# Which groups take the second level of a fast matrix scheme, and where their chains begin: a change to a pooled-attention and snake-MLP kernel

## The chip, the cores and the metric

The kernel runs on one core of a Trainium2 chip. The metric is the device time of one execution in microseconds (us), the median of several runs. The kernel before takes 938.45 us (three runs, 937.84 to 940.55).

The engines named in this document are TensorE (PE in the profile, its weight loads PEld), VectorE (DVE), ScalarE (ACT), GpSimd (POOL) and SyncE (SP, which issues nearly all transfers). [...]

## The reference

Attention with keys and values that are pooled by eight, and behind it two matrix products with a "snake" activation between them. All tensors are float32.

```python
# q, k, v: (8, 8, 576, 64)
k_p = k.reshape(B, H, Sp, 8, D).mean(axis=3)          # 72 pooled keys
v_p = v.reshape(B, H, Sp, 8, D).mean(axis=3)
attn = softmax(q @ k_p.T / sqrt(D))
x = (attn @ v_p)                                       # as 4608 tokens of 512
h = x @ w_in                                           # w_in: 512 x 2048
s = sin(alpha * h)
g = h + s * s / (alpha + 1e-9)
out = g @ w_out                                        # w_out: 2048 x 512
```

## The kernel before

The tokens are handled in nine **units** of 512 (u = 0 to 8). In each unit the product `x @ w_in` is taken as a 2 x 2 block product by a scheme that needs seven products instead of eight. The 2048 columns are taken in four **groups** (J = 0 to 3), and a group goes through seven **slots** (k = 0 to 6) with the products 1, 5, 6, 2, 7, 3, 4. One product is four matmuls of 128 x 128 by 256 columns. TensorE accumulates the scheme's sums in four PSUM banks of the group, b1, b6, b5, b7; copies on ScalarE carry a partial sum from one bank to the next (b1 to b6, b6 to b7), and additions on VectorE close the four results.

Beside this the attention of the next batch is spread over the slots as "extras": scores, shifts (maximum and subtraction, VectorE), exponentials (ScalarE), normalisation (VectorE sums, GpSimd multiplies), turning of blocks by 32 x 32 transposes (VectorE) and moves by SyncE.

In units 1 to 6 (`two`) some products go through **the scheme a second time**: product 5 in groups 1, 2 and 3, and product 1 in group 3. Such a product is seven matmuls of 128 columns where the plain form has four of 256, and needs three copies on ScalarE and one addition on VectorE of its own:

```python
def a():
    products((1, 5), (y[:, 0], y[:, 1]), True)                    # TensorE, into bank y
    nc.scalar.copy(out=f[:, 0], in_=y[:, 0:1].to_broadcast([P, 2, P]))
    m5[p] = self.sm.tile([P, 1, P], F32, name=f"m{p}", bufs=1)
    nc.scalar.copy(out=m5[p][:], in_=y[:, 1:2])
def b():
    products((6, 2), (c[1], c[0]))
    nc.scalar.copy(out=c[2], in_=c[1])
def d():
    products((7,), (c[2],))
    nc.vector.tensor_tensor(out=f[:, :, 1], in0=x, in1=m5[p][:].to_broadcast([P, 2, P]), op=OP.add)
def e():
    products((3, 4), (c[1], c[2]))
```

The parts of a group that the steps below follow, in the order of the program (G is this group, Q the one in front of it, N the next one when it is begun early, which is so for group 3; cuts are marked):

```python
if k == 0:
    ...
        self.last_sines(Q, 2 if not inner else 0)
    extras()
    ...
    if G.i5: G.i5.a()
    if G.i1: self.last_sines(Q, 0)
    else:
        product(G, 1, G.b1, True)
        if G.i5: product(Q, 4, Q.b7, part=(2, 3))
elif k == 1:
    if not G.i1: copy(G.b6[:], G.b1[:])
    if G.i5 and not G.i1:
        self.last_sines(Q, 1); G.i5.b()
    ...
    extras()
    if not G.i5: product(G, 5, G.b5, True)
...
elif k == 3:
    copy(G.b7[:], G.b6[:])
    G.p5 = self.tp.tile([P, JW, TH], F32, name="p5")
    if not G.i5: copy(G.p5[:], G.b5[:])
    else:
        if G.i1: squares(Q, 0)
        squares(Q, 1)
        G.i5.d()
        self.finish(Q); self.store_g(Q)
    extras()
    product(G, 2, G.b1)
    if G.i1: G.i5.e(); copy(G.p5[:], G.b5[:])
elif k == 4:
    sin(G, 0, 0, G.b1)
    ...
    extras()
    product(G, 7, G.b7, part=(0, 1))
    if G.i5:
        if not G.i1: G.i5.e(); copy(G.p5[:], G.b5[:])
        square(G, 0, 0)
    product(G, 7, G.b7, part=(2, 3))
elif k == 5:
    add(G.g[:, 1, :, 1], G.b7[:], G.p5[:])       # VectorE: reads b7 and p5
    extras()
    ...
    product(G, 3, G.b6)
else:
    add(G.g[:, 0, :, 1], G.b6[:], G.p5[:])
    sin(G, 1, 1, G.g[:, 1, :, 1])
    last()                                       # VectorE: b1 + s
    extras()
    product(G, 4, G.b7, part=(0, 1))             # writes b7 again
    ...
```

In units 1 to 6 the extras of group 1 hold the exponentials (slots 8, 9, 10, 10), the normalisations (10, 10, 11, 12) and the turns (12, 12, 13, 13). The extras of group 3 hold the turning of a later batch's q (`turn_q`: parts 0 and 1 on VectorE in slots 22 and 23, parts 2 and 3 as transfers in 24 and 25) and the attention's product with the values (`all_values`, slot 25).

Of the kernel before, what the change touches and what calls it, by code (L numbers as in the profile page):

```python
# [40 lines left out]
class Kernel:  # L41
# [704 lines left out]
    def inner_w_in(self):  # L746

        w = self.q_tile(0)[:]
        at = 0
        for p, J0 in ((5, 1), (1, 3)):  # L750
            n = self.NJ - J0
            A = self.A[p][:].rearrange("p k (J j m) -> p k J j m", j=2, m=P)[:, :, J0:]
            L = lambda i, j: A[:, j, :, i]
            s1, s2, s3, s4 = (w[:, at + i * n * P:at + (i + 1) * n * P].rearrange("p (J m) -> p J m", m=P) for i in range(4))
            at += 4 * n * P
            self.sums(((s1, L(1, 0), L(1, 1), OP.add), (s2, s1, L(0, 0), OP.subtract), (s3, L(0, 0), L(1, 0), OP.subtract), (s4, L(0, 1), s2, OP.subtract)))
            self.W2[p] = J0, {1: L(0, 0), 2: L(0, 1), 3: s4, 4: L(1, 1), 5: s1, 6: s2, 7: s3}
# [25 lines left out]
    def hidden(self, u, extra):  # L783

        nc = self.nc
        add = lambda o, x, y: nc.vector.tensor_tensor(out=o, in0=x, in1=y, op=OP.add)  # L786
        copy = lambda o, x: nc.scalar.copy(out=o, in_=x)  # L787
        sin, square, early = self.sin, self.square, lambda G: G.J == (0 if G.u else 1)
        two = 0 < u < self.B - 1

        def begin(J):

            b1, b6, b5, b7 = (self.bank([P, JW, TH]) for _ in range(4))
            new = lambda n, **kw: self.hp.tile([P, 2, JW, 2, TH], F32, name=n, **kw)
            G = SimpleNamespace(u=u, J=J, b1=b1, b5=b5, b6=b6, b7=b7, g=new("h"), s=self.s,
                                p5=None, i1=None, i5=None, early=J == (0 if u else 1))
            if two and J > 0:
                G.i5 = self.inner_product(G, 5, b5, 7)
            if two and J == 3:
                G.i1 = self.inner_product(G, 1, b1, 6)  # L800
            return G

        def product(G, p, ps, start=False, part=range(4)):

            xT, bt = self.xT[G.u], self.bt[G.u]
            B = lambda i, j: xT[:, 2 * i:2 * i + 2, j * TH:(j + 1) * TH]
            x = {1: B(0, 0), 2: B(1, 0), 3: B(1, 1), 4: bt[:, 3], 5: bt[:, 0], 6: bt[:, 1], 7: bt[:, 2]}[p]
            for n in part:
                jj, kk = divmod(n, 2)
                f = G.J * JW + jj  # L810
                nc.tensor.matmul(ps[:, jj, :], self.A[p][:, kk, f * P:(f + 1) * P], x[:, kk, :],  # L811
                                 start=(start and n == 0), stop=(kk == 1), skip_group_check=True)

        def squares(Q, i):

            if i == 0 and not Q.early:
                square(Q, 0, 1)
            if i == 1:
                square(Q, 1, slice(0, 2))

        self.squares = squares
        for slot in range(7 * self.NJ):
            J, k = divmod(slot, 7)
            Q, G = self.before, self.group

            def extras():
                for f in extra[slot]:
                    f()

            if k == 0:  # L830
                Q = self.before = G
                N = self.next
                inner = N or (two and J > 0)
                if Q and not N:
                    self.last_sines(Q, 2 if not inner else 0)
                extras()
                G = self.group = N or begin(J)
                self.next = None
                if G.i5:
                    G.i5.a()  # L840
                if G.i1:
                    self.last_sines(Q, 0)
                else:
                    product(G, 1, G.b1, True)
                    if G.i5:
                        product(Q, 4, Q.b7, part=(2, 3))
            elif k == 1:
                if not G.i1:
                    copy(G.b6[:], G.b1[:])
                if G.i5 and not G.i1:  # L850
                    self.last_sines(Q, 1)
                    G.i5.b()
                if Q and not G.i1:
                    squares(Q, 0)
                    if not G.i5:
                        squares(Q, 1)
                extras()
                if not G.i5:
                    product(G, 5, G.b5, True)
            elif k == 2:  # L860
                if Q and not G.i5:
                    self.finish(Q)
                extras()
                if G.i1:
                    product(G, 6, G.b6, part=(0, 1))
                    G.i5.b()
                    self.last_sines(Q, 1)
                    product(G, 6, G.b6, part=(2, 3))
                else:
                    product(G, 6, G.b6)  # L870
            elif k == 3:
                late = J == 0 and two
                if Q and not late and not G.i5:
                    self.store_g(Q)
                copy(G.b7[:], G.b6[:])
                G.p5 = self.tp.tile([P, JW, TH], F32, name="p5")
                if not G.i5:
                    copy(G.p5[:], G.b5[:])
                else:
                    if G.i1:  # L880
                        squares(Q, 0)
                    squares(Q, 1)
                    G.i5.d()
                    self.finish(Q)
                    self.store_g(Q)
                extras()
                product(G, 2, G.b1)
                if G.i1:
                    G.i5.e()
                    copy(G.p5[:], G.b5[:])  # L890
            elif k == 4:
                sin(G, 0, 0, G.b1)
                if not G.i5:
# [4 lines that stand above are left out]
                    if not G.i1:  # L898
                        G.i5.e()
                        copy(G.p5[:], G.b5[:])  # L900
# [3 lines that stand above are left out]
                add(G.g[:, 1, :, 1], G.b7[:], G.p5[:])  # L904
                extras()
                N = None
                if two and J + 1 == 3:
                    N = self.next = begin(J + 1)
                    N.i1.a()
                product(G, 3, G.b6, part=(0, 1))  # L910
                if N:
                    N.i1.b()
                product(G, 3, G.b6, part=(2, 3))
            else:
                if J == 0 and two and Q:
                    self.store_g(Q)
                add(G.g[:, 0, :, 1], G.b6[:], G.p5[:])
                sin(G, 1, 1, G.g[:, 1, :, 1])
                N = self.next
                last = lambda: add(G.g[:, 0, :, 0], G.b1[:], G.s[:, 0, :, 0])  # L920
                if not N:
                    last()
                    extras()
                    product(G, 4, G.b7, part=(0, 1))
                    if not (two and J < 3):
                        product(G, 4, G.b7, part=(2, 3))
                else:
                    product(G, 4, G.b7, part=(0,))
                    N.i1.d()
                    last()  # L930
                    product(G, 4, G.b7, part=(1, 2))
                    N.i1.e()
                    copy(N.b6[:], N.b1[:])
                    extras()
                    product(G, 4, G.b7, part=(3,))
# [165 lines left out]
    def carry(self, u):  # L1101
# [3 lines left out]
        at = lambda slot, f, *a: x[slot].append(lambda: f(*a))  # L1105
        last = self.B - 1
        b = u + 1
        if u == 0:
            A0, A = self.att[:2]
# [43 lines left out]
            turn = 23  # L1153
# [3 lines left out]
        if 0 < u < last:  # L1157
            A = self.att[b]
# [2 lines left out]
            at(6, A.two_shifts)  # L1161
            for i in range(4):
                at((8, 9, 10, 10)[i], A.exp, i)
                at((10, 10, 11, 12)[i], A.norm, i)
                at((12, 12, 13, 13)[i], A.turn, i)
            at(14, A.move, range(4))
            at(6, self.load_v, b)
# [11 lines left out]
            turn = 22  # L1179
        elif u:  # L1180
            turn = None
        if turn and u + 2 <= last:
            for part in range(4):
                at(turn + part, self.turn_q, u + 2, part)
        if u + 1 < self.NU:
            at(27, self.sums_of_x, u + 1, 0)
            at(27, self.sums_of_x, u + 1, 1)
# [325 lines left out]
```

## Time and profile before

| | |
|---|---|
| time | 938.45 us (937.84 to 940.55) |
| span of the profiled execution | 938.6 us |
| TensorE matmuls busy | 910.1 us, 97% |
| VectorE busy | 678.7 us, 72% |
| ScalarE busy | 452.0 us, 48% |
| GpSimd busy | 205.7 us, 22% |
| mean TensorE clock granted | 0.991 of full speed |

In the trace a matmul of 128 x 128 by 256 float32 columns leaves two matmul records, so a product of four matmuls appears as "x8". A record's own duration is longer than its share of a stream[...]; the pace is read from the start of one group of records to the start of the next. In a timeline line the first number is the start in us from the span's start, the second is how long the merged group took, and the bracket says how long the engine sat idle in front of it and what released it.

The units with the second level lie between about 91 us and 452 us of the span; one of them takes some 60 us (product with the next scores begins at 94.54, 154.82, 215.43 and 276.27 us).

### The profile page before, as it was taken

How to read it: one execution, taken by the hardware profiler on the slowest of the kernel's cores; microseconds unless marked ns; L12 is line 12 of the kernel's file. 1: busy time of each engine (PE TensorE's matmuls, PEld its weight loads, DVE VectorE, ACT ScalarE, POOL GpSimd, SP SyncE). 2: the span in 40 equal slices, each digit the busy share in tenths (PEclk: the TensorE clock that was granted, in tenths of full speed). 3: DMA queues.
4: the chain of work that ended last, by engine and by line, in shares of the span. 5: the costliest groups of instructions: out<-in, count | busy, mean ns of one | idle time of the engine just before them, and what ended most of it. 6: DMA issues, size and time to landing. Idle time of an engine off the chain costs nothing.

```text
span 938.6 us, 18229 instructions
## 1 busy us (share of the span) xinstructions
PE 910.1 (97%) x7146; PEld 821.0 (87%) x7146; DVE 678.7 (72%) x1030; ACT 452.0 (48%) x1070; POOL 205.7 (22%) x215
## 2 busy tenths in 40 slices
PE   8999999999998999999999999999999999999997
PEld 5787778788777787778888899999999999999997
DVE  6685666656767467564446889988889798989795
ACT  5686665866667767666796641212111111211111
POOL 4788352624624346231000000000000000000000
PEclk9999999999999999999999999999999999999999
DMA  9965766757647575444725445353435444352501
GB/s 247 241 192 154 194 167 182 179 167 173 198 148 200 166 184 159 148 147 120 258 90 168 163 141 162 92 164 90 157 97 136 118 127 128 112 142 90 163 15 38
DMA packets 134796, 141.15 MB, mean 150 GB/s; under 512 B 49896, under 2 KB 103288, under 8 KB 134712
## 3 DMA queue, kind: packets, MB, share of 16 engines
q1 hardware_dynamic: 132536, 138.03, 51.9%
q10 hardware_dynamic: 2176, 1.97, 0.8%
q8 instruction: 57, 0.93, 0.4%
q14 instruction: 27, 0.22, 0.1%
HBM read 75.37 MB, written 47.19 MB: 131 GB/s over the span
## 4 chain that ended last, share of the span: by engine, by line
PE 79%; ACT 7%; DVE 4%; DMA 3%; SPq 3%; issue 2%; POOL 1%; ACTq 0%; DVEq 0%; POOLq 0%
PE PS L1258 40%; PE PS L811 31%; PE PS L971 2%; PE PS L291 2%; SPq L492 2%; PE PS L579 2%; ACT s L948 1%; ACT s L941 1%; ACT ex L340 1%; DMA a<-in_moe_w_in_dram 1%; DMA h<-in_v_dram 1%; DVE h L993 1%; PE PS L592 1%; ACT L340 1%; DVE h L786 1%
## 5 line engine op out<-in xcount | busy, mean ns | idle before, releaser
L811 PE MATMUL PS<-home,a 128*128 128x256 f32 x1104 | 267.3, 388 | 14.9 <-DVE h L786 13.8
L811 PEld LDWEIGHTS PS<-home,a 128*128 128x128 f32 x1104 | 206.6, 194 | 51.7 <-DVE h L786 16.6
L811 PE MATMUL PS<-home,as 128*128 128x256 f32 x720 | 171.4, 382 | 0.4 <-ACT PS L787 0.4
L811 PEld LDWEIGHTS PS<-home,as 128*128 128x128 f32 x720 | 132.5, 190 | 18.2 <-issue 1.3
L1258 PE MATMUL PS<-s,wb 128*128 128x144 f32 x896 | 119.3, 286 | 0.4 <-ACT PS L1378 0.4
L1258 PEld LDWEIGHTS PS<-s,wb 128*128 128x128 f32 x896 | 113.7, 190 | 0.7 <-ACT PS L1378 0.6
L948 ACT ACTIVATE s<-s,c 128x256 f32<-128x256 f32 (+1 forms) x216 | 111.2, 579 | 0.0
L786 DVE TENSOR_TENSOR h<-PS,p 128x512 f32<-128x512 f32 x72 | 49.1, 683 | 73.1 <-PE PS L811 44.1
L941 ACT ACTIVATE s<-h,al 128x256 f32<-128x256 f32 x144 | 65.6, 510 | 58.5 <-DVE h L786 55.0
L122 POOL TENSOR_TENSOR kvin<-kvin 96x768 f32<-96x768 f32 (+3 forms) x42 | 72.4, 1724 | 70.6 <-DMA kvin<-in_v_dram 68.9
L1378 ACT COPY PS<-PS 128x144 f32<-128x144 f32 x56 | 14.7, 263 | 145.7 <-PE PS L1258 144.3
L1258 PE MATMUL PS<-r,wb 128*128 128x144 f32 x512 | 73.2, 286 | 0.0
L1258 PE MATMUL PS<-s,a 128*128 128x144 f32 x512 | 73.2, 286 | 0.0
L993 DVE TENSOR_TENSOR h<-PS,s 128x512 f32<-128x512 f32 x36 | 24.8, 688 | 64.2 <-ACT s L948 64.2
L941 ACT ACTIVATE s<-PS,al 128x256 f32<-128x256 f32 x144 | 60.3, 471 | 21.9 <-PE PS L811 20.4
L1258 PEld LDWEIGHTS PS<-r,wb 128*128 128x128 f32 x512 | 67.1, 190 | 0.1
L1258 PEld LDWEIGHTS PS<-s,a 128*128 128x128 f32 x512 | 67.0, 190 | 0.0
L787 ACT COPY PS<-PS 128x512 f32<-128x512 f32 x72 | 41.4, 575 | 39.1 <-PE PS L811 28.2
L1397 ACT COPY PS<-PS 128x144 f32<-128x144 f32 x56 | 14.7, 263 | 88.4 <-PE PS L1258 88.4
L1258 PE MATMUL PS<-s,we 128*128 128x144 f32 x384 | 54.9, 286 | 0.0
L1258 PE MATMUL PS<-x,wb 128*128 128x144 f32 x384 | 54.9, 286 | 0.0
L993 DVE TENSOR_TENSOR h<-h,s 128x1024 f32<-128x1024 f32 x36 | 51.0, 1417 | 0.0
(214 smaller groups left out, 1397.8 us busy)
## 6 DMA issues: line engine op xcount, KB each, us to landing
g_bridge<-h SPq DMA_DIRECT2D x72, 512.0 KB
r<-g_bridge SPq DMA_DIRECT2D x31, 1152.0 KB
out_dram<-o SPq DMA_DIRECT2D x124, 72.0 KB
kvin<-in_k_dram SPq DMA_DIRECT2D x14, 576.0 KB
q<-in_q_dram SPq DMA_DIRECT2D x7, 1024.0 KB
kvin<-in_v_dram SPq DMA_DIRECT2D x14, 512.0 KB
aM<-tr SPq DMA_DIRECT2D x54, 92.0 KB
aM<-tr SPq DMA_DIRECT2D x54, 88.0 KB
```

The source lines that it names most:

```text
L122: self.nc.gpsimd.tensor_tensor(out=t[..., 0:w] if w > D else out, in0=t[..., 0:w], in1=t[..., w:2 * w], op=OP.add)
L291: nc.tensor.matmul(ps[e][r0 + r:r0 + r + q.shape[-1], h, :], q[s], kb[s, hp, :], start=True, stop=True)
L340: nc.scalar.activation(out=E(i), in_=E(i), func=AF.Exp, scale=scale)
L492: queue.dma_start(out=self.aM[r:r + 32, a, 0:w], in_=tr[32 * a:32 * a + 32, c, s, 0:w])
L579: nc.tensor.matmul(o[r:r + 64], w, x, start=start and i < 2, stop=False, skip_group_check=True)
L786: add = lambda o, x, y: nc.vector.tensor_tensor(out=o, in0=x, in1=y, op=OP.add)
L787: copy = lambda o, x: nc.scalar.copy(out=o, in_=x)
L811: nc.tensor.matmul(ps[:, jj, :], self.A[p][:, kk, f * P:(f + 1) * P], x[:, kk, :], start=(start and n == 0), stop=(kk == 1), skip_group_ch ...
L941: self.nc.scalar.activation(out=G.s[:, i, jj, j, :], in_=src[:, jj], func=AF.Sin, scale=self.al[:, f:f + 1])
L948: self.nc.scalar.activation(out=x, in_=x, func=AF.Square, scale=self.c[:, f:f + 1])
L993: add = lambda o, x, y: self.nc.vector.tensor_tensor(out=o, in0=x, in1=y, op=OP.add)
L1258: nc.tensor.matmul(out, W[:, J // 2, J % 2, :], A[:, J, :], start=(start and J == 0), stop=(J == self.NJ - 1), skip_group_check=True)
```

## The change

The change has five parts.

1. **Group 1 of units 1 to 6 goes back to the plain form of product 5.** Only groups 2 and 3 keep the second level. The sums of the weights for it are made for two groups instead of three.
2. **What hangs on it in group 0 and group 1:** the second half of product 4 of group 0 stays in its own slot 6 and is no longer put behind product 1 of group 1; the last sines of group 0 all come in slot 7; product 5's copy into `p5` comes in slot 10, ahead of that slot's extras.
3. **One normalisation is begun a slot earlier** (the first in slot 9 instead of 10).
4. **Product 5's chain of group 3 begins in group 2:** step a in slot 20, between parts of product 4 of group 2; b in slot 21, d in slot 23 between the halves of product 6, and e where it was, behind product 2.
5. **The turning of q stands behind the addition of step d:** both VectorE parts in slot 23, and that slot's extras behind d.

Parts 1 to 3 take the second level's copies and late closing out of the group that also carries the exponentials; parts 4 and 5 are to keep the closing of product 5 in group 3 from standing behind the transposes of q.

```diff
@@ inner_w_in
-        for p, J0 in ((5, 1), (1, 3)):
+        for p, J0 in ((5, 2), (1, 3)):
@@ begin(J)
-            if two and J > 0:
+            if two and J > 1:
                 G.i5 = self.inner_product(G, 5, b5, 7)
@@ k == 0
-                inner = N or (two and J > 0)
                 if Q and not N:
-                    self.last_sines(Q, 2 if not inner else 0)
+                    self.last_sines(Q, 0 if two and J == 2 else 2)
                 extras()
                 G = self.group = N or begin(J)
                 self.next = None
-                if G.i5:
-                    G.i5.a()
                 if G.i1:
+                    G.i5.b()
                     self.last_sines(Q, 0)
                 else:
+                    if G.i5:
+                        G.i5.a()
                     product(G, 1, G.b1, True)
@@ k == 2
-                extras()
+                if not G.i1:
+                    extras()
                 if G.i1:
                     product(G, 6, G.b6, part=(0, 1))
-                    G.i5.b()
+                    G.i5.d()
+                    extras()
                     self.last_sines(Q, 1)
                     product(G, 6, G.b6, part=(2, 3))
@@ k == 3
                     squares(Q, 1)
-                    G.i5.d()
+                    if not G.i1:
+                        G.i5.d()
                     self.finish(Q)
@@ k == 6
                     product(G, 4, G.b7, part=(0, 1))
-                    if not (two and J < 3):
+                    if not (two and J == 1):
                         product(G, 4, G.b7, part=(2, 3))
                 else:
                     product(G, 4, G.b7, part=(0,))
                     N.i1.d()
                     last()
+                    N.i5.a()
                     product(G, 4, G.b7, part=(1, 2))
@@ carry: the extras of units 1 to 6
-                at((10, 10, 11, 12)[i], A.norm, i)
+                at((9, 10, 11, 12)[i], A.norm, i)
@@ carry: turning of q
-                at(turn + part, self.turn_q, u + 2, part)
+                at(((turn, turn + 1) if u == 0 else (23, 23))[part] if part < 2 else turn + part, self.turn_q, u + 2, part)
```

## The prediction

> **What bounds the kernel now.** I read the page first. TensorE's matmuls are busy for 910.1 us of 938.6, so about 28 us are open gaps. A second loss hides inside the busy time: the mean granted clock is 0.991. Then I asked who ends TensorE's waits. One line carries half of the gaps.
>
> ```profile
> L811 PE MATMUL PS<-home,a 128*128 128x256 f32 x1104 | 267.3, 388 | 14.9 <-DVE h L786 13.8
> ```
> ```profile
> PE PS L811 <- DVE h L786: 13.8, 7, 2.3
> PE PS L971 <- DVE PS L986: 2.4, 2, 1.4
> ```
>
> The second fence is the list of TensorE's waits: us in total, times, longest. The reader is to see that 13.8 us come in seven waits, the longest 2.3. In the timeline of TensorE alone, six of them are exactly 2.25 us, at 117.51, 177.79, 238.40, 299.25, 359.22 and 419.78 us: one in each of units 1 to 6, always ahead of the first half of product 4 in group 1. The seventh is 0.26 us in unit 0. So this is one place in the program, not jitter. The timeline of all engines in unit 2 shows the chain:
>
> ```profile
> 170.74 0.58 ACT L787 COPY PS<-PS 128x512 f32<-128x512 f32 x1
> 171.25 1.33 ACT L948 ACTIVATE s<-s,c 128x512 f32<-128x512 f32 x2
> 172.49 1.48 ACT L340 ACTIVATE ex<-ex 128x576 f32<-128x576 f32 x2
> ...
> 173.99 1.28 ACT L941 ACT_TABLE_LOAD   x1
> ...
> 175.28 0.84 ACT L941 ACTIVATE s<-PS,al 128x256 f32<-128x256 f32 x2
> ...
> 176.01 0.58 ACT L787 COPY p<-PS 128x512 f32<-128x512 f32 x1
> ...
> 177.04 0.69 DVE L786 TENSOR_TENSOR h<-PS,p 128x512 f32<-128x512 f32 x1
> ```
>
> Read it backwards. Product 4 writes b7, so it waits for the addition b7 + p5 (177.04). That waits for the copy into p5 (176.01). The copy stands in ScalarE's order behind two exponentials, a table load and two sines, because step e of the second level ends only in slot 11. ScalarE is 48% busy over the span, but in this stretch it is full: 12.85 us busy of 15.80 (162.00 to 177.80). The bound here is ScalarE's order, although the page calls the kernel TensorE bound.
>
> The wait has a tail. Two stretches right behind it, in units 1 and 2, from one table by stretches (columns: length, busy time of PE, PEld, DVE, ACT, POOL, then the clock):
>
> ```profile
> 117.50:122.00 4.50, 4.17 (x20) 3.40 (x20) 4.47 (x10) 2.06 (x6) 2.67 (x3) 1.00 1.03 275
> 177.80:183.50 5.70, 5.70 (x21) 4.91 (x22) 5.67 (x14) 2.82 (x7) 3.79 (x4) 0.70 0.88 230
> ```
>
> In unit 2 the clock behind the wait is 0.70 in the mean, which is 0.30 x 5.70 / 0.5 = 3.4 us at half speed. From the start of that product 4 to step b of group 2 it takes 183.47 - 177.79 = 5.68 us; in unit 1 it takes 122.06 - 117.51 = 4.55, of which 0.39 is a further wait. The slow clock costs 5.68 - 4.16 = 1.52 us. Units 3, 5 and 6 look like unit 2 (5.69, 5.62, 5.67), unit 4 like unit 1.
>
> In group 3 step e waits for the addition of step d, which stands behind the transposes of q, and these wait for a move to free their buffer (unit 1):
>
> ```profile
> 136.48 3.02 DVE L214 STREAM_TRANSPOSE tr<-q 128x1024 f32<-128x1024 f32 x4 [3.28 <-DMA aM<-tr]
> ...
> 139.88 0.49 PE L971 MATMUL PS<-home,q 128*128 128x128 f32 x2 [1.38 <-DVE PS L986]
> ```
>
> [...] Here the load takes 1.28 us and the sines start right behind it (173.99 to 175.28)[...]. [...]
>
> **The change part by part.** Paces first: 16 records of 128x256 take 3.45 us from start to start (87.46 to 90.94, less a few ns), so 0.216 us a record; a pair of 128-column records takes 0.222 us.
>
> *Product 5 of group 1.* Plain: 8 x 0.216 = 1.73 us. Second level: 7 x 0.222 = 1.55. All of it lies on TensorE's path: +0.18 us a unit, +1.1 us in six.
>
> *Removed from ScalarE in group 1:* copies of 0.36, 0.26 and 0.28 us, on the chain; from VectorE, one addition of 0.43.
>
> *The chain of group 1 anew, on unit 2's clock,* from the start of product 4 of group 0 at 163.16. TensorE without waits: product 4 to 164.89, product 1 to 166.62, 5 to 168.35, 6 to 170.08, 2 to 171.81, 7 to 173.54, 3 to 175.28. ScalarE, by the steps between starts in the trace: sines at 164.08 (they wait for the addition at 163.36, which does not move), square 164.90, sines of b7 165.70, copy to b6 when product 1 has landed, 166.85, squares 167.33, table load 168.57, first two exponentials 169.85, copy to b7 171.01 to 171.59, p5 to 172.0, the third exponential to 172.7, the fourth to 173.5. So b7 is ready for product 7 (171.81). VectorE: the third normalisation's sum waits for 172.7 and ends at 173.6; the addition b7 + p5 waits for product 7 (about 173.74) and ends at 174.43. TensorE wants b7 at 175.28: **the wait is gone with 0.85 us to spare**.
>
> *Into group 2.* In unit 1 step b waits for a copy that comes 5.26 us after that addition began (116.80 to 122.06). Now 173.74 + 5.26 = 179.00, and TensorE arrives at 175.28 + 3.89 = 179.17: the 0.39 wait goes too. The copy to b6 ends about 0.1 us late for product 6, at 179.7.
>
> *Sum of the stretch* from product 4 of group 0 to product 6 of group 2. Before: 19.87 us (unit 1), 20.75, 20.76, 19.88, 20.71, 20.75. After: 72 records x 0.216 + 4 pairs x 0.222 + 0.1 = 16.5. Saved 3.3 us twice and 4.2 four times: 23.5 us, the 1.1 already paid. Four slow-clock stretches of 1.52 are 6.1 of it; six waits of 2.25 are 13.5; the rest is small stalls.
>
> *Group 3.* From product 4 of group 2 to product 7 of group 3 the units take 12.61, 12.17, 12.20, 12.30, 12.17 and 12.17 us before. The step-e wait (1.38 in unit 1, 1.07 in unit 4, 0.44 on the weight loads in unit 5) disappears: step d's addition now ends at about 5.0 us after that product 4 begins, and step e arrives at 7.0. But the next limit is close. The product with the values needs the bank that VectorE's `finish` reads, and in unit 2 its weight load waits 1.02 us for it:
>
> ```profile
> 201.15 0.20 PEld L579 LDWEIGHTS PS<-aM,vm 64*64 64x64 f32 x4 [1.02 <-DVE h L993]
> ```
>
> `finish` waits for the squares. I put these at 8.2 us after product 4 begins, since the copy to b7 comes 0.1 later than before; the transposes of q, now behind the addition, end at 5.0 + 3.02 = 8.0. So group 3 takes about 12.3 us everywhere: -0.3 in unit 1, +0.1 in four. **I count zero.** GpSimd's weight sums for group 1 are hidden.
>
> **The rivals.** *The exponentials become the limit of b7's addition through VectorE.* The normalisations stand ahead of the addition. If the third exponential ends a microsecond later than I chain it, product 4 waits 0.2 us or more a unit; an ideal 23.5 becomes 19 only if that is 0.75 us in every unit. For: ScalarE stays full in group 1. Against: the move of one normalisation to slot 9 and three copies fewer. *The slow clock stays.* If it belonged to phases of the run and not to the wait, 6 us stay lost and the result is 921. Against: it appears only behind the wait. *Group 3 pays it back.* If the move of the blocks lands 1 us later against TensorE, `finish` and the values slip in five units: 5 us, 921. Against: the turns on VectorE begin 0.7 us earlier against TensorE than before. *Only the matmuls count:* +1.1 us, 939.5; the six waits speak against it.
>
> **Range and chances.** The ideal is 938.45 - 23.5 = 915. I allow 0.25 us a unit for stalls that the chain does not show: 1.5 us, so **916.5 us**. One rival coming true gives about 921, two give 925; the best case with group 3 also shorter is 913. I take 913 to 922 as the range of 8 in 10. Faster by over 2% means below 919.7: 0.8; within 2%: 0.19; slower: 0.01.
>
> **What would show it.** In the changed profile the wait of product 4 on the addition should have left the list of TensorE's waits; the granted clock of units 1 to 6 should be 1.00 in every stretch, the mean near 0.998 (0.991 plus 4 x 3.4 x 0.5 / 938.6); one unit should take 57 us instead of 60.5; the p5 copy of group 1 should stand ahead of the exponentials; step e in group 3 should wait for nothing, and the weight load of the values should wait about 1.1 us for `finish` also in units 1 and 4. Wrong I would be if product 4 of group 1 still waited, now behind the normalisations; if half-speed stretches stayed; or if the values in group 3 waited 2 us.

## The result, and the profile after

The changed kernel takes 918.44 us (four runs, 916.87 to 918.86) against 938.42 us before. The ratio is 0.978 (95% interval 0.9761 to 0.9799): faster by 2.2%. In the profiled executions the span falls from 938.6 to 916.9 us.

The list of TensorE's waits, changed kernel (us in total, times, longest):

```profile
PE PS L579 <- DVE h L997: 1.8, 6, 0.3
...
PE PS L811 <- DVE h L786: 0.3, 1, 0.3
```

The 13.8 us in seven waits are 0.3 us in one. That one lies in unit 0; of the six in units 1 to 6 nothing is left. What heads the list now was not on it: the product with the values (L579) waits for VectorE in each of the six units. The same stretch of unit 2 as before the prediction, in the timeline of all engines (its clock is 3.81 us earlier: product 4 of group 0 starts at 159.35 instead of 163.16):

```profile
167.30 0.58 ACT L787 COPY PS<-PS 128x512 f32<-128x512 f32 x1
...
167.81 0.58 ACT L787 COPY p<-PS 128x512 f32<-128x512 f32 x1
...
168.29 1.49 ACT L340 ACTIVATE ex<-ex 128x576 f32<-128x576 f32 x2
...
169.96 0.69 DVE L786 TENSOR_TENSOR h<-PS,p 128x512 f32<-128x512 f32 x1
...
171.49 1.03 PE L811 MATMUL PS<-home,a 128*128 128x256 f32 x4
```

The copy into p5 (167.81) now stands ahead of the last two exponentials and the table load. The addition (169.96) ends at 170.65, and product 4 (171.49) has no bracket: it waited for nothing. By stretches (length, busy time of the engines in the order of the table before, then the clock; the last two numbers are the DMA's), units 1 and 2:

```profile
102.00:119.00 17.00, 17.00 (x84) 14.85 (x82) 13.67 (x24) 14.56 (x28) 10.67 (x8) 1.00 0.96 248
159.00:176.00 17.00, 17.00 (x84) 14.73 (x82) 14.03 (x25) 14.84 (x29) 10.88 (x8) 1.00 0.95 237
```

TensorE is busy for all 17.00 us, at a clock of 1.00. The other four units show the clock of 1.00 too, with 16.90 to 17.00 us busy.

### The profile page after: what moved, and what is told of

Read it like the earlier page. It is cut to its first block, busy times and chain, and to the rows that moved or that the text cites. A ratio compares the mean times of both kernels' runs of the same rounds, so it can differ in the third digit from the quotient of the medians.

```text
span 916.9 us, 18121 instructions
## 1 busy us (share of the span) xinstructions
PE 905.1 (99%) x7110; PEld 817.0 (89%) x7110; DVE 675.2 (74%) x1024; ACT 446.4 (49%) x1052; POOL 210.7 (23%) x215
## 4 chain that ended last, share of the span: by engine, by line
PE 83%; DMA 4%; POOL 4%; DVE 3%; ACT 3%; SPq 2%; issue 1%; ACTq 0%; POOLq 0%; DVEq 0%
PE PS L1262 41%; PE PS L811 34%; DMA kvin<-in_v_dram 3%; PE PS L975 3%; ACT s L952 2%; PE PS L579 2%; POOL kvin L122 1%; POOL ex L348 1%; PE PS L291 1%; SPq L646 1%; DVE h L997 1%; PE PS L592 1%; DMA a<-in_moe_w_in_dram 1%; PE PS L1036 0%; POOL as L652 0%
## 5 line engine op out<-in xcount | busy, mean ns | idle before, releaser
L811 PE MATMUL PS<-home,a 128*128 128x256 f32 x1104 | 257.9, 381 | 1.2 <-ACT home L506 0.8
L811 PE MATMUL PS<-home,as 128*128 128x256 f32 x768 | 182.2, 382 | 0.3 <-ACT PS L787 0.3
L811 PEld LDWEIGHTS PS<-home,as 128*128 128x128 f32 x768 | 142.1, 190 | 20.2 <-POOL q L771 0.8
L1262 PEld LDWEIGHTS PS<-s,we 128*128 128x128 f32 x384 | 50.4, 190 | 0.1
```

What stands on the lines that cost most here:

```text
L1262: nc.tensor.matmul(out, W[:, J // 2, J % 2, :], A[:, J, :], start=(start and J == 0), stop=(J == self.NJ - 1), skip_group_check=True)
```

## The experiments

All ratios are to the kernel before, timed beside it on the same chip.

**Which part carries the gain.** The yardstick is the changed kernel once more:

> The changed kernel once more, as the yardstick for the runs beside it. All theories: 918.4 us, 0.978 of the kernel before, no half-speed stretch in units 1 to 6.

919.66 us, ratio 0.9787 (0.9773 to 0.9801). Beside it, parts 1 to 3 alone:

```diff
@@ on the kernel before
-        for p, J0 in ((5, 1), (1, 3)):
+        for p, J0 in ((5, 2), (1, 3)):
-            if two and J > 0:
+            if two and J > 1:
-                inner = N or (two and J > 0)
-                    self.last_sines(Q, 2 if not inner else 0)
+                    self.last_sines(Q, 0 if two and J == 2 else 2)
-                    if not (two and J < 3):
+                    if not (two and J == 1):
-                at((10, 10, 11, 12)[i], A.norm, i)
+                at((9, 10, 11, 12)[i], A.norm, i)
```

> Parts 1 to 3 alone, group 3 as before. My theory (group 1 carries the whole gain, group 3 is bound by squares and finish and gives nothing): 918.4 us, within 1 us of the changed kernel. Rival (the chain begun early in group 3 carries a share): 921 us or more, with waits of step e behind the transposes in most units.

918.15 us, ratio 0.9773 (0.9760 to 0.9787): no slower than the whole change. Step e does wait behind the transposes in three units, up to 1.37 us, but the values that follow then wait less, as the prediction said of group 3. Parts 4 and 5 alone:

```diff
@@ on the kernel before; group 1 keeps its second level
+                    N.i5.a()                        # at the start of group 3, behind its i1.d and last()
@@ k == 0, in the branch of group 3
-                if G.i5:
-                    G.i5.a()
+                    G.i5.b()
@@ k == 2, in the branch of group 3; k == 3 keeps i5.d for the other groups alone
-                extras()
-                    G.i5.b()
+                    G.i5.d()
+                    extras()
@@ requests: parts 0 and 1 of turn_q in slot 23 for all units but the first
-                at(turn + part, self.turn_q, u + 2, part)
+                at(((turn, turn + 1) if u == 0 else (23, 23))[part] if part < 2 else turn + part, self.turn_q, u + 2, part)
```

> Parts 4 and 5 alone, group 1 keeps the second level. My theory: 938 us, the six waits of 2.25 us ahead of product 4 and the half-speed stretches are all there. Rival (group 3 carries a share): 935 us or less.

939.74 us, ratio 1.0003 (0.9995 to 1.0012). The six waits are all there. So group 1 carries the whole gain and the change in group 3 gives nothing that these runs can see.

Part 3 needed no run of its own: with the first normalisation in slot 10 or in slot 9, every engine gets its instructions in the same order, since nothing else of that engine's lies between the two places. It moves a line of the program, not an instruction. So the argument in the prediction that a normalisation moves forward counts for nothing.

**Is it ScalarE's order?** In the changed kernel, group 1's copy into p5 goes back behind the sines of slot 11:

```diff
@@ k == 3
                 if not G.i5:
-                    copy(G.p5[:], G.b5[:])
+                    if not (two and J == 1):
+                        copy(G.p5[:], G.b5[:])
@@ k == 4
                 sin(G, 0, 0, G.b1)
+                if two and J == 1:
+                    copy(G.p5[:], G.b5[:])
```

> The changed kernel, but group 1's copy into p5 stands behind the sines of slot 11 again, as it did before; no second level in group 1. My theory (ScalarE's order holds product 4 up through the addition): the copy ends about 2 us later than now, the addition b7 + p5 starts about 1.6 us later, product 4 waits about 1.0 us in each of six units and group 2 begins late too: 924 to 927 us. Rival (the second level itself, its own work and chain, was what cost): 918 to 919 us, no wait. If the half-speed stretches come from any wait of this length, some return and it is 927 to 930.

930.24 us, ratio 0.9902 (0.9888 to 0.9916). Unit 2 in the timeline:

```profile
172.78 0.59 ACT L787 COPY p<-PS 128x512 f32<-128x512 f32 x1
...
173.40 0.69 DVE L786 TENSOR_TENSOR h<-PS,p 128x512 f32<-128x512 f32 x1 [2.36 <-ACT p L787]
...
174.15 1.13 PE L811 MATMUL PS<-home,a 128*128 128x256 f32 x4 [1.06 <-DVE h L786]
```

With no second level in group 1, one late copy is enough: VectorE sits idle for 2.36 us until it is done, and product 4 waits 1.06 us. The whole costs more than I expected, 10.6 us over the yardstick: the six waits of 1.06 us are 6.4 of it, step b of group 2 waits another 0.44 us in each unit, and the remaining 1.6 us were not traced. No half-speed stretch came back: the mean clock of the profiled execution is 0.999.

**Is it only ScalarE's order?** The second level returns to group 1, but there step e and the copy into p5 come ahead of the slot's exponentials:

```diff
@@ k == 3, in the changed kernel with the second level back in group 1
+                if G.i5 and J == 1:
+                    product(G, 2, G.b1)
+                    G.i5.e()
+                    copy(G.p5[:], G.b5[:])
                 extras()
-                product(G, 2, G.b1)
+                if not (G.i5 and J == 1):
+                    product(G, 2, G.b1)
```

> The changed kernel with the second level back in group 1, but there step e and the copy into p5 come ahead of that slot's exponentials. Theory of the prediction (the late p5 copy on ScalarE is what holds the addition up): the wait of 2.25 us shrinks to 0.3 us or goes, 918 to 921 us. Rival (VectorE's own queue holds the addition up as well: finish starts late behind the squares, and three normalisations stand between it and the addition without a gap): the addition stays where it was, product 4 waits 2 us or more, 934 to 938 us.

932.79 us, ratio 0.9934 (0.9919 to 0.9950). Between the two theories, and the timeline of unit 2 says why:

```profile
171.25 0.56 ACT L787 COPY p<-PS 128x512 f32<-128x512 f32 x1
171.38 0.69 DVE L1002 TENSOR_TENSOR h<-PS,s 128x512 f32<-128x512 f32 x1 [1.00 <-ACT s L957]
...
173.11 0.75 DVE L346 TENSOR_REDUCE sm<-ex 128x8 f32<-128x584 f32 x1
...
174.89 0.68 DVE L786 TENSOR_TENSOR h<-PS,p 128x512 f32<-128x512 f32 x1
...
175.62 1.13 PE L811 MATMUL PS<-home,a 128*128 128x256 f32 x4 [1.02 <-DVE h L786]
```

The copy into p5 is done by 171.81, three microseconds ahead of the addition (174.89), which has no bracket: VectorE came to it late from its own queue. `finish` (171.38) had waited for the squares on ScalarE, and two normalisations (173.11 and the next) stand between it and the addition. So the late copy was one of two chains of nearly equal length. In the kernel before, the copy ended at 176.59. `finish` began there only at 172.61, again behind the squares, and VectorE's queue reached the addition at 177.04 with no idle time behind the end of `finish` (174.44):

```profile
172.61 0.69 DVE L993 TENSOR_TENSOR h<-PS,s 128x512 f32<-128x512 f32 x1 [2.53 <-ACT s L948]
173.22 1.22 DVE L993 TENSOR_TENSOR h<-h,s 128x1024 f32<-128x1024 f32 x1
...
174.35 0.75 DVE L346 TENSOR_REDUCE sm<-ex 128x8 f32<-128x584 f32 x1
```

**Can the second level stay if all of it is put in order?** A first try also brings squares and `finish` forward and puts the second exponential behind the copy, where the third and fourth already stand:

```diff
@@ on top of the last one
-                    if not G.i5:
+                    if not G.i5 or J == 1:          # k == 1: squares of the group in front
                         squares(Q, 1)
-                if Q and not G.i5:
+                if Q and (not G.i5 or J == 1):      # k == 2: finish
                     self.finish(Q)
-                at((8, 9, 10, 10)[i], A.exp, i)
+                at((8, 10, 10, 10)[i], A.exp, i)
```

> As keep_p5, and the squares and finish of the group in front come ahead of all exponentials but for none, so that VectorE is free earlier; three of the four exponentials move behind the copy into p5. Both theories of keep_p5: the wait goes though the second level stays, since it is order and not the second level that counts: 917 to 920 us (0.18 us of matmul a unit less than the changed kernel, against short waits for the copy to b7). Rival (the second level costs more in copies than it saves on TensorE, in any order): 925 us or more.

937.63 us, ratio 0.9984 (0.9975 to 0.9993). The number is in the rival's range, but the rival's reason, "in any order", is not shown by it: product 4 waited only 0.3 us, but step d's addition now stood behind `finish` and a normalisation on VectorE, and step e waited for it, 1.57 to 2.31 us in the six units. Unit 2:

```profile
172.11 0.49 PE L982 MATMUL PS<-home,q 128*128 128x128 f32 x2 [2.01 <-DVE PS L997]
```

The second try puts that addition ahead of both:

```diff
@@ on top of the last one
-                if Q and (not G.i5 or J == 1):      # k == 2
+                if Q and not G.i5:
                     self.finish(Q)                  # group 1: again at k == 3, behind G.i5.d()
-                at((9, 10, 11, 12)[i], A.norm, i)
+                at((10, 10, 11, 12)[i], A.norm, i)
```

> As keep_all (second level kept in group 1, squares early, p5 copy ahead of three exponentials), but step d's addition now stands ahead of finish and of every normalisation on VectorE; in keep_all it stood behind finish and one normalisation and step e waited 1.6 to 2.3 us for it. Theory (it is the order on ScalarE and VectorE that counts, and the second level can stay): step e waits for nothing, product 7 about 0.4 us for the copy to b7, product 4 for nothing: 918 to 921 us. Rival (with the second level in the group that carries the exponentials some step always ends last, in any order): one more wait of a microsecond or more in group 1, 925 us or more.

924.87 us, ratio 0.9846 (0.9833 to 0.9860). The wait of product 4 is gone and the second level is still there. The time lies between the two expectations, but no wait of a microsecond is left in group 1, so the rival's account fails. Most of the change's gain (a ratio of 0.9846 against the yardstick's 0.9787) is thus a matter of order. The rest was not recovered: what stays are three shorter waits in each unit, here in unit 2, for the copy to b7 and for step a's copy (and the copy to b6 behind it):

```profile
168.81 1.99 PE L811 MATMUL PS<-home,a 128*128 128x256 f32 x8 [0.26 <-ACT PS L787]
...
176.96 0.49 PE L981 MATMUL PS<-last,q 128*128 128x128 f32 x2 [0.39 <-ACT PS L985]
177.28 0.39 PE L981 MATMUL PS<-home,as 128*128 128x128 f32 x2
177.64 1.99 PE L811 MATMUL PS<-home,as 128*128 128x256 f32 x8
```

From product 4 of group 0 to product 6 of group 2 unit 2 takes 177.64 - 159.92 = 17.72 us here and 16.60 in the changed kernel. I tried no further order; whether one exists that makes the second level pay in group 1 stays open. It could save at most the 0.18 us a unit that the matmuls differ by.

**The next limit.** In the changed kernel the values' weight load waits for `finish`. Product 7 is put ahead of the values in group 3:

```diff
@@ k == 4
-                extras()
+                if not G.i1:
+                    extras()
                 product(G, 7, G.b7, part=(0, 1))
+                if G.i1:
+                    product(G, 7, G.b7, part=(2, 3))
+                    extras()
```

> The changed kernel, but in group 3 all of product 7 stands ahead of the attention's product with the values. Theory (the values' weight load waits 1.2 us for finish in each of six units, which is the next limit): product 7's 1.73 us cover the wait, 918.4 - 6 x 1.2 = 911 us. Rival (another limit stands close behind, the copies of x on ScalarE or the addition for product 4): 915 to 918 us.

916.86 us, ratio 0.9766 (0.9749 to 0.9783). The wait for `finish` left the list, and another took most of its place, as the rival said:

```profile
PE PS L253 <- ACT home L506: 6.3, 5, 1.9
```

L253 turns the next batch's pooled keys. It needs a PSUM bank which ScalarE's copies of x (L506) still read. It is wanted only in the next unit's slot 3, so it can go one slot later:

```diff
-                at(26, self.att[b + 1].k_t)
+                at(27, self.att[b + 1].k_t)
```

> As p7_first, and the turning of the next batch's pooled keys (three matmuls and a copy) moves from slot 26 to slot 27. In p7_first these matmuls waited 0.8 to 1.9 us in five units for ScalarE's copies of x, which hold their PSUM bank. Theory (that wait is what took the place of the values' wait): it goes, and the 1.2 us a unit of the values come through: 910 to 912 us. Rival (the copies of x are needed soon by something else as well, so the wait only moves on): 914 to 917 us.

909.54 us (909.19 to 910.61), ratio 0.9682 (0.9669 to 0.9696). Both waits are gone. This version beats both kernels: 3.2% under the kernel before and clear of the changed kernel's interval. Whether parts 4 and 5 help it was not run.

**The clock.** The kernel before once more:

> The kernel before once more, for its clock. My theory [...]: again six waits of 2.25 us, but half-speed stretches behind another number or choice of them than units 2, 3, 5 and 6. Rival (they belong to fixed places of the program): the same four.

939.62 us, span 937.8. The stretches behind the six waits, units 1 to 6:

```profile
117.70:123.40 5.70, 5.69 (x21) 4.96 (x22) 5.67 (x14) 2.84 (x7) 3.79 (x4) 0.70 0.92 232
178.28:184.00 5.72, 5.72 (x21) 4.93 (x22) 5.69 (x14) 2.83 (x7) 3.81 (x4) 0.70 0.86 230
238.89:244.60 5.71, 5.31 (x26) 4.36 (x27) 5.68 (x14) 3.26 (x9) 3.80 (x4) 1.00 0.88 232
298.93:304.60 5.67, 5.28 (x26) 4.33 (x27) 5.64 (x14) 3.23 (x9) 3.76 (x4) 1.00 0.89 232
359.21:364.90 5.69, 5.69 (x21) 4.89 (x22) 5.66 (x14) 2.83 (x7) 3.78 (x4) 0.70 0.87 231
419.83:425.50 5.67, 5.28 (x26) 4.33 (x27) 5.63 (x14) 3.23 (x9) 3.76 (x4) 1.00 0.06 21
```

The clock is 0.70 in units 1, 2 and 5; in the first profile it was units 2, 3, 5 and 6. The same program, the same waits, another choice of stretches: they are not fixed to places in the program.

In the first profile the half-speed stretches begin at 178.24, 239.68, 359.14 and 420.58 us, and each is 3.41 us long. Their starts lie 61.44, 119.46 and 61.44 us apart, which is 18, 35 and 18 times 3.413 us. Units 1 and 2 of that profile, cut with this spacing:

```profile
113.39:116.80 3.41, 1.86 (x9) 1.31 (x7) 3.31 (x8) 3.38 (x7) 1.59 (x2) 1.00 0.52 193
116.80:120.21 3.41, 2.70 (x14) 2.45 (x15) 3.38 (x8) 1.22 (x3) 1.77 (x2) 1.00 1.03 302
...
174.83:178.24 3.41, 1.16 (x6) 0.70 (x5) 3.31 (x8) 3.02 (x8) 2.75 (x3) 1.00 0.86 295
178.24:181.65 3.41, 3.41 (x12) 2.87 (x11) 3.38 (x9) 0.97 (x4) 1.57 (x2) 0.50 1.03 283
```

In unit 1 the wait falls into two of these cuts: TensorE is idle for 1.55 us in one and 0.71 in the next, and the clock stays at 1.00. In unit 2 the whole wait lies in one, 2.25 us idle of 3.41, and the next 3.41 us run at 0.50. The other units of this profile are like these two: ahead of the half-speed stretches of units 3, 5 and 6 TensorE is idle for 2.13, 2.17 and 2.25 us of 3.41, and in unit 4 for 0.72 and 1.53 us in two cuts, with the clock at 1.00 behind both. What sets the spacing, and which of the waits a half-speed stretch follows, was not shown. The length of a wait alone does not tell: keep_all has one of 2.31 us in unit 4, longer than those here, and its profiled execution has a mean clock of 0.999, where a single half-speed stretch of 3.41 us would take off 0.0018 (3.41 x 0.5 / 934.4).

## Why the prediction was right

**The wait of product 4.** Right, and close. On the shifted clock the p5 copy was to end at 172.0, it ended at 168.39 + 3.81 = 172.2; the addition was to start at 173.74 and started at 173.77; product 4 was put at 175.28 and came at 175.30; step b at 179.17 and 179.20; product 6 at 179.7 and 179.76.

**The cause that I named for it** was half of it. I wrote that the addition at 177.04 waits for the copy into p5, and that ScalarE's order was the bound. But that copy had ended 0.45 us earlier, and the addition's line has no bracket: it was held up in VectorE's own queue. late_p5 shows that a late copy is enough for a wait; keep_p5 shows that an early copy does not free product 4, because VectorE's queue, held up by `finish` and the normalisations, is as late. Removing the second level shortened both at once: without it the program puts the squares in slot 8 and no longer in slot 10, and `finish` starts 3.95 us earlier on the same clock (164.85 + 3.81 = 168.66 against 172.61), so that VectorE is free in time:

```profile
164.85 0.69 DVE L997 TENSOR_TENSOR h<-PS,s 128x512 f32<-128x512 f32 x1 [1.96 <-ACT s L952]
```

My chain held this (it put the squares at 167.33 on the old clock, and they came at 163.49 + 3.81 = 167.30), so the numbers came out. The sentence on the bound was too narrow: ScalarE's order delays both chains, but the second one goes on through VectorE's queue, and with an early copy and a late `finish` (keep_p5) 1.02 us of the 2.25 stayed.

**The sum of the stretch.** Predicted 16.5 us in each unit; measured 16.59, 16.60, 16.92, 16.90, 16.59 and 16.84. Saved 122.72 - 100.44 = 22.28 us where the ideal said 23.5. I had allowed 1.5 us for stalls that the chain does not show; it was 1.2. One unit takes 56.7 to 57.2 us, where 57 was predicted. The pace of 0.216 us a record holds in an unbroken stream (147.77 to 151.22, 3.45 us for 16 records); the two starts that I named for it lie 3.48 us apart.

**Group 3.** Predicted about 12.3 us, nothing gained: measured 12.33 or 12.34 in all six units, 74.0 in the sum against 73.62. Step e waits for nothing, as predicted, and the weight load waits for `finish` now in every unit:

```profile
193.45 0.19 PEld L579 LDWEIGHTS PS<-aM,vm 64*64 64x64 f32 x4 [1.19 <-DVE h L997]
```

**The clock.** Predicted 1.00 in the units and 0.998 in the mean; measured 1.00 and 0.999.

**The total** was off by 1.9 us, 916.5 against 918.44, and the term that was wrong is the base of the subtraction. I took 22 us, read off one profiled execution with four half-speed stretches, from the median of 938.45. That execution itself took 940.4 us. From it the same 22 us give 918.4; that this meets the median to 0.1 us is partly luck, since four runs of the changed kernel lie 2.0 us apart. A half-speed stretch is worth 1.1 us (5.68 in unit 2 less 4.55 in unit 1, from product 4 to step b) to 1.5 us (less the 4.16 without a wait), and their number differs between executions of the same program: before_look had three in place of four and took 939.62. That this number makes an execution slow is shown only in part. Of the 27 executions of the kernel before that were timed beside before_look, the ten with a mean clock of 0.991 or 0.992 average 939.7 us and the six with 0.996 average 937.9; in the 17 beside after_again, time and clock do not go together. The parts were sized well, and the wrong base hid in the range.

## What to carry to other kernels

A wait of a few microseconds that recurs once per unit at the same line can be worth more than its own length (here six waits of 2.25 us, 13.5 us, stand against 22.28 us saved in the stretch): follow every operand of the instruction that ends it, not the last one alone, because a second chain may be as late. A scheme that saves 0.18 us of matmul is not free if its copies and additions stand in the queues of the stage where those queues are full. And take a saving that was read off a profile from the time of that profiled execution; here the median would have been 1.95 us off as a base.

## What the runs showed of the hardware that I had not expected

The stalls of 0.3 us in units 3, 4 and 6 go with a slower VectorE addition. `finish`'s second addition has both inputs in SBUF and takes 1.22 us where GpSimd is idle (at 136.59 us in the changed kernel). Where it overlaps GpSimd's first pair of pooling additions in units 1 to 6, it takes 1.31 to 2.20 us; the pair takes 3.71 us in unit 6 and 4.57 or 4.58 in the other five. Unit 3, where both are long, and unit 1 in the changed kernel:

```profile
220.77 4.57 POOL L122 TENSOR_TENSOR kvin<-kvin 128x1024 f32<-128x1024 f32 x2 [11.52 <-DMA kvin<-in_v_dram]
...
222.19 2.02 DVE L997 TENSOR_TENSOR h<-h,s 128x1024 f32<-128x1024 f32 x1
```
```profile
106.60 4.58 POOL L122 TENSOR_TENSOR kvin<-kvin 128x1024 f32<-128x1024 f32 x2 [10.86 <-DMA kvin<-in_v_dram]
...
108.74 1.31 DVE L997 TENSOR_TENSOR h<-h,s 128x1024 f32<-128x1024 f32 x1
```

In units 3, 4 and 6 the addition takes 2.02, 1.99 and 2.20 us, in the others 1.31 to 1.40. What makes it slower, and that the delayed addition caused the stalls in these three units, was not tested by a run.

And the same wait can have a half-speed stretch behind it or not: in three profiles with the 2.25 us wait (both of the kernel before, and group3_only), 10 of 18 waits were followed by one (a clock of 0.70 or 0.71 in the 5.7 us behind the wait), 8 were not (1.00). Behind the twelve waits of product 4 of 1.02 and 1.06 us in keep_p5 and late_p5, whose profiled executions have mean clocks of 1.000 and 0.999, there was none.
